# Gated linear attention with a cosine-gated MLP on one core: another order of the written-out steps behind the first 150

## The chip, the core and the metric

The kernel runs on one core of a Trainium2 chip. The metric is the device time of one execution in microseconds (us). A core has five queues that matter here: PE (matmuls), DVE, ACT and POOL (elementwise work; ACT also holds the tables for exp, ln and sine, POOL cannot read PSUM here) and SP, which only issues transfers. Each queue takes its instructions strictly in the order in which the program wrote them; between queues, semaphores make an instruction wait for its operands and for a free buffer. Matmul results go to PSUM, which the kernel divides into eight banks of 128 x 512 float32.

## The reference

For 4 batches, 8 heads, 768 steps and head width 48, with `state` of 48 x 48 per batch and head:

```python
for t in range(S):
    state = alpha[:, :, t, :, None] * state + np.einsum('bhd,bhe->bhde', k[:, :, t], v[:, :, t])
    y[:, :, t] = np.einsum('bhd,bhde->bhe', q[:, :, t], state)
...
h = x @ w_in            # x: y as 3072 tokens x 384;  w_in: 384 x 2048
g = h * np.cos(h)
return g @ w_out        # w_out: 2048 x 384
```

Inputs and output are float32; the kernel multiplies in bfloat16 and accumulates in float32.

## The kernel before, in words

The 3072 tokens are cut into 12 blocks of 256, J = 0 to 11; three blocks in a row belong to one batch. Inside a block there are two chunks of 128 tokens, and two tokens that follow each other lie on one partition (the index e = 0, 1). The recurrence is done chunk by chunk: with cumulative sums of ln(alpha), keys are scaled by exp(-sum) and queries by exp(sum); inside a chunk the masked products of queries and keys are applied to v, and a state handed from chunk to chunk adds the rest. The result is the MLP's input.

All work is cut into named steps, each for one J (and for one half, chunk or part). The prediction uses these names, "outer 2" being step outer of block 2, "evy 3 1" evy of block 3 with chunk 1, "m2 5 0 3" the second matrix of block 5, chunk 0, part 3:

- SP: `load a/k/q/v` (one input of a block, 384 KB; line 102), `vst` (four small transfers that stack v; 64 KB each), `out` (one output tile of 128 x 384).
- POOL: `mula` (product of neighbouring alphas), `castv` (v to bfloat16; line 219), `decay`, `state` (the decayed new state), and those of `sk` and `sq` (scaled keys and queries, half e) that have no `:D`.
- ACT: `sin` (cosine of a part of h), `eb` (a session: exp(-sum) and exp(sum) of both halves, then ln of the next block; line 203), and evictions marked as ACT's. Going from exp/ln to sine or back loads a table.
- DVE: `gate` (h times cosine), `mask` (scores times the mask), `add` (new state sum), `sub`, and the evictions and scalings marked `:D`.
- Evictions, on ACT or DVE: `evT` (transposed q and k of a chunk), `evy` (y), `evo` (output tile), `vev`.
- PE: `cums` (the sums), `trans` (32 transposes: keys, then queries), `scores` (chunk c), `outer` (state products; two chunks, one in a batch's last block), `yT`, `m1` (first matrix, part u of 4), `m2` (second matrix, chunk c, part p of 4), `vpe` (v restacked, blocks 0 to 2).

The data flow of a block is: loads, mula, ln, cums, sub and eb, sk and sq, trans, evT, scores, mask, yT, evy, then four times m1, sin, gate, then eight m2, two evo, two out. `outer` needs sk and castv; add and state follow it, and yT needs the state.

The order is written out by hand, not found by a scheduler at build time. `PLAN` (line 432) holds for each step and J a number, with a letter for the engine of an eviction or scaling; the steps are sorted by this number alone (line 513) and written in that order, each into its engine's queue. The numbers are not times that anything waits for. A step that stands early in a queue and has to wait holds up all that stands behind it in that queue.

Buffers set the other waits. Six PSUM banks form a ring "h" of three two-bank tiles (line 172), taken in turn by trans, scores, outer, yT and m1: the fourth of them waits until the first is evicted. Two more banks stand alone: "x" for cums and vpe, "o" for the output tiles of m2. Of input tiles there are three per tensor (four of alpha; `BUF`, line 45), of output tiles in SBUF four, so the fifth evo waits until the first tile is stored. All loads behind the first nine wait for the yT of block 1 (line 99), so that the weights come first.

Of the kernel before, what the change touches and what calls it, by code (L numbers as in the profile page):

```python
# [16 lines left out]
def kernel(  # L17
# [10 lines left out]
    nc = tc.nc  # L28
# [130 lines left out]
    def cums(J):  # L159
        if (J, 1) not in cums_ps:  # L160
            cums_ps[J, 1] = ps.tile([C, 512], FP, tag="x", name="cums", bufs=1)
# [10 lines left out]
    def two_banks(name):  # L172
        return ps.tile([C, 2, 512], FP, tag="h", name=name, bufs=3)

# [56 lines left out]
    def stack_v_pe(J, c):  # L231
        vs_ps[J, c] = ps.tile([C, 512], FP, tag="x", name="vs_ps", bufs=1)
        for e in range(2):
            r, o = slice(HC * c, HC * c + HC), slice(HC * e, HC * e + HC)
            nc.tensor.matmul(vs_ps[J, c][o, 0:HD].rearrange("s (h d) -> s h d", h=H), ident_bf[r, r],
                             vp_t[J % NV][r, e, :, 0:D], start=True, stop=True)
# [45 lines left out]
    def outer(J):  # L282
        n = 2 if J % NJB < NJB - 1 else 1
        kh, vp = kh_t[J % NQ], vp_t[J % NV]
        U_ps[J] = two_banks("U_ps")
        for p in range(NP):
            for e in range(2):
                for c in range(n):
                    r = slice(HC * c, HC * c + HC)
                    nc.tensor.matmul(  # L290
                        U_ps[J][:, c, 2 * p * D : 2 * (p + 1) * D].rearrange("r (a d) -> r a d", a=2),
# [7 lines left out]
    def add_state(J, c):  # L299
        n = 2 * J + c  # L300
        us = sb.tile([C, NP, 2, D], FP, tag="us", name="us", bufs=BUF["us"])
        s = U_ps[J][:, c, 0:HD].rearrange("r (p a d) -> r p a d", p=NP, a=2)
# [13 lines left out]
    def yT(J):  # L316
        y_ps[J] = two_banks("y_ps")
# [20 lines left out]
        for z, (c, g, i, l, r) in enumerate(todo):  # L338
            last = nc.tensor.matmul(y_ps[J][32 * g : 32 * g + 32, c, i * C : (i + 1) * C], l, r,  # L339
# [6 lines left out]
    def evict_y(J, c, copy):  # L346
        if J not in xT:
# [3 lines left out]
             in_=y_ps[J][:, c, 0 : KT * C].rearrange("r (i e t) -> r i e t", i=KT, e=2))  # L351
# [24 lines left out]
    def mlp2(J, c, part):  # L376
        if (J, c) == (NJ - 1, 1):
            if part == 0:

                o_ps[J, c] = [ps.tile([C, 512], FP, tag="x", name="o_last", bufs=1), two_banks("o_last")[:, 0]]  # L380
# [5 lines left out]
        if part == 0:  # L386
            o_ps[J, c] = ps.tile([C, 512], FP, tag="o", name="o_ps", bufs=1)
# [23 lines left out]
    def idle(n):  # L411
        if not idle_ps:
            idle_ps.append(ps.tile([C, 512], FP, tag="o", name="idle_ps", bufs=1))
# [7 lines left out]
        "mula": mul_a, "ln": ln, "cums0": cums0, "cums": cums, "sub": sub, "icp": icp, "exps": exps, "eb": session,  # L421
        "sk": lambda J, e, eng="POOL": scale_k(J, e, mults[eng]), "sq": lambda J, e, eng="POOL": scale_q(J, e, mults[eng]),
        "castv": cast_v, "vst": stack_v, "vpe": stack_v_pe,
# [3 lines left out]
        "m1": mlp1, "sin": cosine, "gate": gate, "m2": mlp2, "evo": lambda J, c, eng="ACT": evict_o(J, c, copies[eng]),  # L427
# [118 lines left out]
```

## Time and profile before

| what | us |
| --- | --- |
| median of 3 runs | 183.99 (183.46 to 184.06) |
| span of the profiled execution | 182.3 |
| PE busy | 175.4 |
| DVE busy | 134.8 |
| ACT busy, 18 table loads of 1.28 among it | 129.9 |
| POOL busy | 71.4 |
| bytes moved | 29.47 MB, mean 162 GB/s |

The profiled execution's own time is known as its span, from the first to the last instruction; it is 1.7 us less than the median of the runs. In the profile, a line such as `L389 PE MATMUL o_ps<-w,gsb` names the line of the kernel, the engine, the operation and the tiles (output, then inputs). The chain of waits lists, in order of time, start, length and what ran or was waited for. The timeline lists start, duration, engine, line, operation and tiles, and in brackets the idle time before it with what ended it. Matmuls overlap, so the durations of neighbours may not be added; the distance from start to start is what one takes from PE. In the trace PE names its tiles: `T_ps` is trans, `A_ps` scores, `U_ps` outer, `y_ps` yT, `h_ps` m1, `o_ps` m2; on the others `gsb` is gate, `c_sb` sin, `kh` and `qh` sk and sq, `xT` evy, `qkT` evT, `us` add, `un` state, `vp` castv.

### The profile page before, as it was taken

The page shows a single profiled execution, that of the slowest core. Times are in us where ns is not written, and L with a number is a line of the kernel's source. Part 1 is how long each engine was busy: PE and PEld are TensorE (multiplying, and loading weights), DVE is VectorE, ACT ScalarE, POOL GpSimd, SP SyncE. Part 2 cuts the span into 40 slices and gives each one's busy share as a digit, 9 for nine tenths or more (in the row PEclk, how much of TensorE's full clock was granted, in tenths as well). Part 3 has the DMA queues.
Part 4 walks back from the last instruction along what each step waited for, and adds up shares of the span by engine and source line. Part 5 has one row for each costly group of instructions (what it writes and reads, how often), then busy time and mean ns, then how long its engine had stood idle before and what let it go on. Part 6 is the DMA issues. An engine that isn't in the chain of part 4 may idle for free.

```text
span 182.3 us, 5756 instructions
## 1 busy us (share of the span) xinstructions
PE 175.4 (96%) x2467; PEld 132.6 (73%) x2470; DVE 134.8 (74%) x183; ACT 129.9 (71%) x169; POOL 71.4 (39%) x104
## 2 busy tenths in 40 slices
PE   7999899989999999998999999999999999999993
PEld 2455789746697877975799669686876796787872
DVE  7188878678879897599889886978688778363460
ACT  2837687998989999959578999838964174383331
POOL 5145830377777103734894298240720320100000
PEclk9999999999999999999999999999999999999999
DMA  5999999999989959996629905690052142010032
GB/s 148 261 261 220 199 215 221 273 260 265 248 184 283 249 132 295 289 277 202 147 63 229 273 18 166 155 233 0 4 110 83 45 109 81 4 43 4 0 129 86
DMA packets 57801, 29.47 MB, mean 162 GB/s; under 512 B 50992, under 2 KB 56496, under 8 KB 57776
## 3 DMA queue, kind: packets, MB, share of 16 engines
q1 hardware_dynamic: 56256, 25.86, 58.3%
q0 software_dynamic: 1376, 3.15, 9.3%
q8 instruction: 19, 0.31, 0.7%
q10 hardware_dynamic: 144, 0.10, 0.2%
q14 instruction: 6, 0.05, 0.1%
HBM read 25.17 MB, written 4.72 MB: 164 GB/s over the span
## 4 chain that ended last, share of the span: by engine, by line
PE 77%; ACT 11%; DVE 6%; DMA 2%; issue 2%; ACTq 0%
PE h_ps L360 29%; PE o_ps L389 28%; PE y_ps L339 5%; DVE gsb L371 5%; PE idle_ps L415 4%; ACT c_sb L366 3%; PE A_ps L273 3%; PE T_ps L259 3%; DMA a<-in_alpha_dram 2%; PE U_ps L290 2%; ACT L366 2%; PE o_last L383 1%; ACT L137 1%; ACT lna L142 1%; PE cums_h L156 1%
## 5 line engine op out<-in xcount | busy, mean ns | idle before, releaser
L371 DVE TENSOR_TENSOR gsb<-h_ps,c_sb 128x1024 bf16<-128x1024 f32 x48 | 58.2, 1222 | 20.8 <-ACT c_sb L366 19.4
L366 ACT ACTIVATE c_sb<-h_ps,halfpi 128x1024 bf16<-128x1024 f32 x48 | 53.3, 1115 | 26.7 <-PE h_ps L360 26.4
L389 PE MATMUL o_ps<-w,gsb 128*128 128x384 bf16 x368 | 67.1, 327 | 0.6 <-DVE o_sb L401 0.6
L360 PE MATMUL h_ps<-xT,w 128*128 128x256 bf16 x576 | 67.0, 273 | 0.3 <-issue 0.2
L360 PEld LDWEIGHTS <-w 128*128 128x128 bf16 x576 | 62.4, 114 | 2.5 <-DMA w<-in_moe_w_in_dram 0.3
L389 PEld LDWEIGHTS <-gsb 128*128 128x128 bf16 x368 | 33.9, 98 | 21.4 <-issue 1.1
L312 POOL TENSOR_TENSOR un<-us,c 128x384 bf16<-128x384 f32 x20 | 16.8, 838 | 46.2 <-DVE us L304 36.9
L278 DVE TENSOR_TENSOR A_sb<-A_ps,msk 128x1024 bf16<-128x1024 f32 x24 | 28.9, 1216 | 3.4 <-PE A_ps L273 3.4
L217 POOL TENSOR_TENSOR qh<-q,cp 128x384 bf16<-128x384 f32 x13 | 13.8, 1063 | 13.3 <-ACT cp L201 12.2
L213 POOL TENSOR_TENSOR kh<-k,icp 128x384 bf16<-128x384 f32 x15 | 14.9, 1007 | 2.4 <-ACT icp L193 1.0
L220 POOL CAST vp<-v 128x768 bf16<-128x768 f32 x12 | 9.9, 827 | 12.0 <-DMA v<-in_v_dram 12.0
L150 POOL TENSOR_TENSOR a<-a 128x384 f32<-128x384 f32 x9 | 9.0, 1003 | 10.1 <-DMA a<-in_alpha_dram 10.1
L142 ACT ACTIVATE lna<-a 128x768 bf16<-128x768 f32 x12 | 10.1, 844 | 3.5 <-DMA a<-in_alpha_dram 3.3
L415 PE MATMUL idle_ps<-zeros 128*128 128x512 bf16 x38 | 11.1, 439 | 1.4 <-DVE halfpi L77 1.2
L401 ACT COPY o_sb<-o_ps 128x384 f32<-128x384 f32 x13 | 6.2, 478 | 8.5 <-PE o_ps L389 8.5
L137 ACT ACT_TABLE_LOAD x9 | 11.5, 1283 | 0.9 <-PEq L530 0.7
L366 ACT ACT_TABLE_LOAD x9 | 11.5, 1283 | 0.2
L304 DVE TENSOR_TENSOR us<-U_ps,un 128x384 f32<-128x384 f32 x16 | 8.8, 551 | 3.8 <-POOL un L312 2.1
L265 ACT COPY qkT<-T_ps 128x1024 bf16<-128x1024 bf16 x10 | 9.8, 1016 | 1.9 <-PE T_ps L259 1.8
L217 DVE TENSOR_TENSOR qh<-q,cp 128x384 bf16<-128x384 f32 x11 | 6.8, 629 | 5.4 <-DMA q<-in_q_dram 5.3
L265 DVE COPY qkT<-T_ps 128x1024 bf16<-128x1024 bf16 x14 | 9.4, 680 | 1.2 <-PE T_ps L259 1.2
L273 PE MATMUL A_ps<-qkT 48*128 48x128 bf16 x192 | 9.0, 217 | 0.7 <-DVE gsb L371 0.5
(70 smaller groups left out, 156.6 us busy)
## 6 DMA issues: line engine op xcount, KB each, us to landing
a<-in_alpha_dram SPq DMA_DIRECT2D x12, 384.0 KB, 5.9
q<-in_q_dram SPq DMA_DIRECT2D x12, 384.0 KB, 6.1
k<-in_k_dram SPq DMA_DIRECT2D x12, 384.0 KB, 6.0
v<-in_v_dram SPq DMA_DIRECT2D x12, 384.0 KB, 6.3
out_dram<-o_sb SPq DMA_DIRECT2D x23, 192.0 KB, 3.5
vs<-vp SPq DMA_DIRECT2D x36, 64.0 KB, 2.8
w<-in_moe_w_in_dram POOLq DMA_DIRECT2D x2, 768.0 KB, 9.6
w<-in_moe_w_out_dram POOLq DMA_DIRECT2D x4, 384.0 KB, 8.7
```

The source lines that it names most:

```text
L137: nc.scalar.preload_act_table_set("natural_log_exp_and_others")
L213: eng.tensor_tensor(out=kh_t[J % NQ][:, e, :, 0:D], in0=kqv["k", J][:, :, e], in1=icp_, op=ALU.mult)
L217: eng.tensor_tensor(out=qh_t[J % NQ][:, e, :, 0:D], in0=kqv["q", J][:, :, e], in1=cp, op=ALU.mult)
L265: copy(out=qkT_sb[J][:, c], in_=T_ps[J][:, c].rearrange("r n e s -> r n (e s)"))
L273: nc.tensor.matmul(A_ps[J, c][:, a, p, :], qkT[r, c, NP + p, :], qkT[r, c, p, :], start=True, stop=True)
L278: nc.vector.tensor_tensor(out=A_sb[J][:, c].rearrange("s a p t -> s (a p) t"), in0=A_ps.pop((J, c)).rearrange("s a p t -> s (a p) t"), in1 ...
L312: nc.gpsimd.tensor_tensor(out=u, in0=U_sum.pop(n), in1=c2_sb[J][:, :, c].unsqueeze(3).to_broadcast([C, NP, 2, D]), op=ALU.mult)
L360: nc.tensor.matmul(h_ps[J, u][:, f, :], cols, xT[J][:, kk, :], start=(kk == 0), stop=(kk == KT - 1))
L366: nc.scalar.activation(out=c_sb[J, u], in_=h_ps[J, u], func=AF.Sin, bias=halfpi, scale=1.0)
L371: nc.vector.tensor_tensor(out=gsb[J][:, u * FW : (u + 1) * FW], in0=h_ps.pop((J, u)), in1=c_sb.pop((J, u)), op=ALU.mult)
L389: nc.tensor.matmul(o_ps[J, c][:, 0:DM], gsb[J][:, ft, c * C : (c + 1) * C], w2[:, ft], start=(ft == 0), stop=(ft == NF - 1))
L415: nc.tensor.matmul(idle_ps[0], zeros[:, 0:C], zeros, start=True, stop=True)
```

## The change

The order of the first 150 steps stays: up to about 40 us of the profile. Their numbers are new, ranks in place of the old ones. Behind them all steps are put in another order, on every queue, the loads and stores included. Three things go with it:

- Nine steps carry the mark `X` and use the other one of the two single banks: vpe 2 0 in "o"; m2 5 1, m2 7 1, m2 8 1, m2 9 0 and m2 10 1 in "x"; the state products outer 3, 10 and 11 leave the ring "h" and take "x" and "o" (block 11 only "x").
- 26 evictions change engine: twelve go from ACT to DVE (evT 3 1, 9 1, 10 0, 11 1; evy 2 1, 4 1, 8 1, 11 0; evo 1 1, 3 1, 6 0, 8 0) and fourteen from DVE to ACT (evT 6 1, 8 0, 10 1, 11 0; evy 5 1, 7 0, 7 1, 8 0, 9 0, 9 1; evo 4 1, 7 0, 8 1, 10 0).
- Two entries of w1 that did nothing are dropped.

No step is added or removed, and none changes its size. The start of the new part, on PE (old, then new):

```
old: m2 1 0 1, trans 2, outer 2, vpe 2 1, m2 1 0 2, vpe 2 0, scores 2 1, m2 1 0 3, cums 4, trans 3, scores 2 0,
     m2 1 1 0, m2 1 1 1, scores 3 0, m2 1 1 2, yT 2, scores 3 1, outer 3, m2 1 1 3, cums 5, m1 2 1 ...
new: trans 2, m2 1 0 1, m2 1 0 2, m2 1 0 3, outer 2, scores 2 1, vpe 2 0, vpe 2 1, scores 2 0, trans 3, cums 4,
     m2 1 1 0, m2 1 1 1, m2 1 1 2, m2 1 1 3, yT 2, scores 3 1, scores 3 0, outer 3, m1 2 0 ...
```

On POOL:

```
old: sk 2 1, castv 2, sk 3 1, sq 3 0, state 2 0, mula 5, castv 3, decay 3, sk 4 1, sk 4 0, ...
new: sk 2 1, sk 3 1, castv 2, decay 3, sq 3 0, mula 5, castv 3, state 2 0, sk 4 1, sq 4 0, ...
```

On SP, behind load v 3:

```
old: k4 q4 a6 a7 v4 vst3 k5 q5 out(0,1) out(0,0) q6 a8 a9 vst4 a10 out(1,1) q7 k6 v5 ...
new: k4 a6 q4 v4 vst3 k6 q5 k5 a9 v5 q6 out(0,0) a7 a8 out(0,1) vst4 v7 v6 out(1,0) k7 ...
```

The diff, with the reading sides of the changed tiles (`[:, c, ...]` becomes `[c][:, ...]`) and some rows of the plan left out:

```diff
--- before.py
+++ after.py
@@ -156,9 +156,12 @@
             nc.tensor.matmul(o, m.rearrange("p c i -> p (c i)"), lna_t[J % NL][:, i, :, 0:D], start=(i == 0),
                              stop=(i == len(mats) - 1))
 
-    def cums(J):
+    def one_bank(name, tag):
+        return ps.tile([C, 512], FP, tag=tag, name=name, bufs=1)
+
+    def cums(J, tag="x"):
         if (J, 1) not in cums_ps:
-            cums_ps[J, 1] = ps.tile([C, 512], FP, tag="x", name="cums", bufs=1)
+            cums_ps[J, 1] = one_bank("cums", tag)
         t = cums_ps[J, 1]
         lna = lna_t[J % NL]
         ne = 1 if J in both else 2
@@ -172,6 +175,12 @@
     def two_banks(name):
         return ps.tile([C, 2, 512], FP, tag="h", name=name, bufs=3)
 
+    def two(name, apart, n=2):
+        if apart:
+            return [one_bank(name, tag) for tag in ("x", "o")[:n]]
+        t = two_banks(name)
+        return [t[:, c] for c in range(2)]
+
     def cums0(J):
         t = two_banks("cums_h")
         for e in range(2):
@@ -228,8 +237,8 @@
 
     vs_ps = {}
 
-    def stack_v_pe(J, c):
-        vs_ps[J, c] = ps.tile([C, 512], FP, tag="x", name="vs_ps", bufs=1)
+    def stack_v_pe(J, c, tag="x"):
+        vs_ps[J, c] = one_bank("vs_ps", tag)
         for e in range(2):
             r, o = slice(HC * c, HC * c + HC), slice(HC * e, HC * e + HC)
             nc.tensor.matmul(vs_ps[J, c][o, 0:HD].rearrange("s (h d) -> s h d", h=H), ident_bf[r, r],
@@ -279,16 +288,16 @@
             out=A_sb[J][:, c].rearrange("s a p t -> s (a p) t"), in0=A_ps.pop((J, c)).rearrange("s a p t -> s (a p) t"),
             in1=msk.rearrange("s e2 t -> s (e2 t)").unsqueeze(1).to_broadcast([C, H, C]), op=ALU.mult)
 
-    def outer(J):
+    def outer(J, other=""):
         n = 2 if J % NJB < NJB - 1 else 1
         kh, vp = kh_t[J % NQ], vp_t[J % NV]
-        U_ps[J] = two_banks("U_ps")
+        U_ps[J] = two("U_ps", other, n)
         for p in range(NP):
             for e in range(2):
                 for c in range(n):
                     r = slice(HC * c, HC * c + HC)
                     nc.tensor.matmul(
-                        U_ps[J][:, c, 2 * p * D : 2 * (p + 1) * D].rearrange("r (a d) -> r a d", a=2),
+                        U_ps[J][c][:, 2 * p * D : 2 * (p + 1) * D].rearrange("r (a d) -> r a d", a=2),
                         kh[r, e, 2 * p : 2 * p + 2, :].rearrange("s h d -> s (h d)"),
                         vp[r, e, 2 * p : 2 * p + 2, 0:D], start=(e == 0), stop=(e == 1))
 
...
@@ -313,8 +322,8 @@
                                 in1=c2_sb[J][:, :, c].unsqueeze(3).to_broadcast([C, NP, 2, D]), op=ALU.mult)
         U_new[n] = u
 
-    def yT(J):
-        y_ps[J] = two_banks("y_ps")
+    def yT(J, other=""):
+        y_ps[J] = two("y_ps", other)
         qkT, A, vs = qkT_sb.pop(J), A_sb.pop(J), vs_t[J % NS]
         todo = []
         for i in range(KT):
...
@@ -373,18 +382,18 @@
 
     HALVES = [slice(0, DM // 2), slice(DM // 2, DM)]
 
-    def mlp2(J, c, part):
+    def mlp2(J, c, part, tag="o"):
         if (J, c) == (NJ - 1, 1):
             if part == 0:
 
-                o_ps[J, c] = [ps.tile([C, 512], FP, tag="x", name="o_last", bufs=1), two_banks("o_last")[:, 0]]
+                o_ps[J, c] = [one_bank("o_last", "x"), two_banks("o_last")[:, 0]]
             for z, cols in enumerate(HALVES):
                 for ft in range(part * NF // MP, (part + 1) * NF // MP):
                     nc.tensor.matmul(o_ps[J, c][z][:, 0 : DM // 2], gsb[J][:, ft, c * C : (c + 1) * C], w2[:, ft, cols],
                                      start=(ft == 0), stop=(ft == NF - 1))
             return
         if part == 0:
-            o_ps[J, c] = ps.tile([C, 512], FP, tag="o", name="o_ps", bufs=1)
+            o_ps[J, c] = one_bank("o_ps", tag)
         for ft in range(part * NF // MP, (part + 1) * NF // MP):
             nc.tensor.matmul(o_ps[J, c][:, 0:DM], gsb[J][:, ft, c * C : (c + 1) * C], w2[:, ft],
                              start=(ft == 0), stop=(ft == NF - 1))
...
@@ -418,86 +427,86 @@
     mults = {"DVE": nc.vector, "POOL": nc.gpsimd}
     steps = {
         "load": lambda J, nm: load(nm, J), "w1": load_w1, "w2": load_w2,
-        "mula": mul_a, "ln": ln, "cums0": cums0, "cums": cums, "sub": sub, "icp": icp, "exps": exps, "eb": session,
+        "mula": mul_a, "ln": ln, "cums0": cums0, "cums": lambda J, other="": cums(J, "o" if other else "x"), "sub": sub, "icp": icp, "exps": exps, "eb": session,
         "sk": lambda J, e, eng="POOL": scale_k(J, e, mults[eng]), "sq": lambda J, e, eng="POOL": scale_q(J, e, mults[eng]),
-        "castv": cast_v, "vst": stack_v, "vpe": stack_v_pe,
+        "castv": cast_v, "vst": stack_v, "vpe": lambda J, c, other="": stack_v_pe(J, c, "o" if other else "x"),
         "vev": lambda J, c, eng="DVE": evict_vs(J, c, copies[eng]), "decay": decay, "trans": trans,
         "evT": lambda J, c, eng="DVE": evict_T(J, c, copies[eng]), "scores": scores, "mask": mask, "outer": outer,
         "add": add_state, "state": decay_state, "yT": yT, "evy": lambda J, c, eng="ACT": evict_y(J, c, copies[eng]),
-        "m1": mlp1, "sin": cosine, "gate": gate, "m2": mlp2, "evo": lambda J, c, eng="ACT": evict_o(J, c, copies[eng]),
+        "m1": mlp1, "sin": cosine, "gate": gate, "m2": lambda J, c, part, other="": mlp2(J, c, part, "x" if other else "o"), "evo": lambda J, c, eng="ACT": evict_o(J, c, copies[eng]),
         "out": store, "idle": idle,
     }
 
 
     PLAN = {
-        "load a": "750 2205 4425 24496 25066 37693 43693 45193 55293 56793 62293 70470",
-        "load k": "3345 7425 31693 34693 40693 52193 64033 73545 85258 93648 94218 114101",
-        "load q": "2775 8925 25636 36193 42193 52763 54533 63463 72180 78488 96723 113531",
-        "load v": "5925 10425 33193 39193 46693 64693 71040 71610 94788 95358 117164 132675",
...
-        "eb": "- - - 39444 47093 58049 68038 83323 88148 102153 108001 126061",
-        "sk 0": "9160:D 14846:D 39112:D 41953:D 48949 58577 77428:D 89268 92888 110613 111733 130015",
-        "sk 1": "9909:D 13739:D 38528 41528 47999 59591:D 73470 88318 91938 107448 124627:D 130965",
...
-        "castv": "12160 17628 40028 46545 56778 71528 75880 90218 100558 104387 129245 144989",
...
-        "trans": "10624 16461 40648 44533 57020 68793 81884 90868 108663 115899 126133 137709",
-        "evT 0": "11929 17161:A 42626:A 45233:A 60041 70290:A 83189 93123 109551 117529:A 130540:A 139589",
-        "evT 1": "11324 18286 41348 46163:A 58511 71220:A 82584 91568 110631 116599:A 131821 138409:A",
...
-        "scores 1": "12159 19026 43154 48677 59649 82364 85716 101272 118725 125913 134675 140410",
...
-        "outer": "14769 19786 41128 48897 68243 85386 81554 104346 116599 118945 140630 151540",
...
-        "yT": "18046 23626 47792 56295 71422 88605 89395 107778 123407 138284 149254 161470",
...
-        "evy 1": "18876 25109 49345 58036:D 72782 89595:D 90795 110156:D 124397 139114:D 150367 162953",
...
-        "m2 1 0": "35362 45328 65536 77529 86551 104771 117324 129332 141275 154809 166285 173504",
...
-        "evo 0": "34574:D 44322 62603 73475 85575 103280:D 116004 128413:D 140515 153925:D 165167:D 176969",
-        "evo 1": "38637:D 54119 68348:D 81659 92173:D 108601:D 123512 133462 144087:D 157621 171423 178295:D",
-        "out 0": "53933 66193 79058 75045 109831 110431 116564 149019 141075 173183 172583 177529",
...
+        "load a": "10 30 60 980 1020 1410 1750 2500 2520 2230 3070 3970",
+        "load k": "50 170 1170 1280 1540 2210 1970 3040 3440 3490 4690 5040",
+        "load q": "40 240 1040 1330 1840 2110 2370 3090 3750 4170 5220 4610",
+        "load v": "100 270 1220 1460 1950 2340 2940 2830 3940 3150 4250 4660",
...
+        "eb": "- - - 1480 1910 2300 2710 3280 3720 4290 4760 4990",
+        "sk 0": "250:D 510:D 1450:D 1500:D 2060 2320 2790:D 3630 4230 4320 4840 5510",
+        "sk 1": "260:D 440:D 1430 1510 1920 2460:D 3190 3670 4050 4640 4910:D 5340",
...
+        "castv": "350 660 1560 1740 2530 3010 3370 3420 4700 4110 4600 5030",
...
+        "trans": "280 610 1520 1730 2250 2770 3320 3800 4750 4770 5570 5560",
+        "evT 0": "330 650:A 1580:A 1870:A 2400 2850:A 3400 3890 4820:A 4860:A 5630 5700:A",
+        "evT 1": "300 690 1530 1800 2310 2900:A 3340:A 3900 4870 4780 5690:A 5650",
...
+        "scores 1": "340 730 1660 1900 2390 3360 3580 4330 4980 5320 5720 5710",
...
+        "outer": "500 790 1610 2000:X 2750 3260 3610 4190 4710 4790 5530:X 5900:X",
...
+        "yT": "680 950 1890 2240 2890 3700 3770 4390 5110 5500 5960 6110",
...
+        "evy 1": "720 1030 1930:D 2350:D 2950:D 3740 3790 4480 5130:D 5600 6060 6170",
...
+        "m2 1 0": "1300 1780 2640 3170 3620 4340:X 4850 5100:X 5610:X 6150 6490:X 6650",
...
+        "evo 0": "1270:D 1630 2590 3120 3540 4470:D 4740:D 5470 6120:D 6400:D 6560 6670",
+        "evo 1": "1440:D 1880:D 2760:D 3350:D 3850 4520:D 5090 5520 5840 6360 6630 6720:D",
+        "out 0": "2490 3030 3220 4150 4620 4800 5590 5850 6200 6420 6600 6700",
...
     }
-    IDLE = [(1201, 9), (6413, 2), (7383, 14), (11727, 1), (12377, 4), (15372, 5), (16939, 5), (20459, 1)]
+    IDLE = [(20, 9), (120, 2), (160, 14), (310, 1), (370, 4), (550, 5), (640, 5), (840, 1)]
 
     order = []
     for key, line in PLAN.items():
@@ -505,7 +514,7 @@
         for J, word in enumerate(line.split()):
             if word != "-":
                 t, _, eng = word.partition(":")
-                args = [J] + [int(x) if x.isdigit() else x for x in rest] + [{"A": "ACT", "D": "DVE", "P": "POOL"}[x] for x in eng]
+                args = [J] + [int(x) if x.isdigit() else x for x in rest] + [{"A": "ACT", "D": "DVE", "P": "POOL", "X": "other bank"}[x] for x in eng]
                 order.append((int(t), len(order), kind, args))
     for t, n in IDLE:
         order.append((t, len(order), "idle", [n]))
```

More of the change, by code (lines that the diff above doesn't have):

```diff
@@ L301, in add_state @@
         us = sb.tile([C, NP, 2, D], FP, tag="us", name="us", bufs=BUF["us"])
-        s = U_ps[J][:, c, 0:HD].rearrange("r (p a d) -> r p a d", p=NP, a=2)
+        s = U_ps[J][c][:, 0:HD].rearrange("r (p a d) -> r p a d", p=NP, a=2)
         if n % (2 * NJB) > 0:
@@ L338, in yT @@
         for z, (c, g, i, l, r) in enumerate(todo):
-            last = nc.tensor.matmul(y_ps[J][32 * g : 32 * g + 32, c, i * C : (i + 1) * C], l, r,
+            last = nc.tensor.matmul(y_ps[J][c][32 * g : 32 * g + 32, i * C : (i + 1) * C], l, r,
                              start=(c, g) not in begun, stop=(c, g, i) not in outs[z + 1 :], skip_group_check=True)
@@ L350, in evict_y @@
         copy(out=xT[J][:, :, c * C : (c + 1) * C].rearrange("r i (t e) -> r i e t", e=2),
-             in_=y_ps[J][:, c, 0 : KT * C].rearrange("r (i e t) -> r i e t", i=KT, e=2))
+             in_=y_ps[J][c][:, 0 : KT * C].rearrange("r (i e t) -> r i e t", i=KT, e=2))
     h_ps, c_sb, o_ps, o_sb = {}, {}, {}, {}
@@ L412, in idle @@
         if not idle_ps:
-            idle_ps.append(ps.tile([C, 512], FP, tag="o", name="idle_ps", bufs=1))
+            idle_ps.append(one_bank("idle_ps", "o"))
         for _ in range(n):
```

94 rows, old and new, of the table PLAN are left out of this document.

## The prediction

> **What bounds the kernel now.** I read the busy table and the slices first, then the chain of waits in order of time, then the timelines of PE, DVE, ACT and POOL around the places where that chain leaves PE.
>
> ```profile
> span 182.3 us, 5756 instructions
> PE 175.4 (96%) x2467; PEld 132.6 (73%) x2470; DVE 134.8 (74%) x183; ACT 129.9 (71%) x169; POOL 71.4 (39%) x104
> PE   7999899989999999998999999999999999999993
> PEclk9999999999999999999999999999999999999999
> ```
>
> PE is the bound, at full granted clock, in every slice behind the start. So a new order can win only two things on PE: waits, and what PE loses between unlike matmuls. The chain shows the second:
>
> ```profile
> 35.87 1.30 PE o_ps L389 x8
> 37.17 0.16 PE cums L156
> ...
> 45.20 1.41 PE o_ps L389 x8
> 46.60 0.33 PE A_ps L273 x8
> 46.93 0.76 PE o_ps L389 x4
> ...
> 68.82 0.23 PE A_ps L273 x8
> 69.04 0.47 PE T_ps L259 x32
> ```
>
> Eight `o_ps` matmuls take 1.30 us ahead of another full-array matmul, 1.41 ahead of scores; eight scores take 0.23 ahead of transposes, 0.33 ahead of `o_ps`. Going from full-array work (cums, m1, m2) to half-row work (trans, scores, outer) or to the column-split yT, or back, costs 0.10 us; among trans, scores and outer it costs nothing. The first is the wait:
>
> ```profile
> 81.83 1.22 DVE gsb L371
> 83.05 0.04 issue
> 83.09 0.40 PE A_ps L273 x8
> ```
>
> **Floor.** Behind step 149, PE runs from 40.03 to 179.27 us in the profile. I laid each PE step at its undisturbed length by the PE timeline (m1 1.31, m2 0.65, trans 0.48, scores 0.23, outer 0.35 or 0.15, yT 0.79 or 0.63, cums 0.26) plus 0.095 for each change of shape. What exceeds it in before by more than 0.05 is waiting: 0.65 between trans 6 and scores 5 1; 0.49 around scores 8 0, outer 8 and cums 11; 0.19 each around scores 6, scores 11 0 and outer 2; 0.15 behind cums 5; 0.11 at m1 3 1. Together 2.0 us.
>
> **The change, part by part.**
>
> Changes of shape: counted along both plans behind step 149, 59 become 50. Nine fewer at 0.10: **-0.9 us**, directly on PE, and nothing hides it.
>
> The waits. I follow each engine's queue in the new order with the durations of the trace (DVE from start to start: gate and mask 1.17, evT 0.60, sk and sq 0.50, other 0.47; ACT: sin 1.11, table load 1.28, a session of icp, exps and ln 2.45).
>
> First new wait, at the seam. POOL's sk 3 1 now stands ahead of castv 2. It needs load k 3:
>
> ```profile
> 40.04 0.82 POOL L220 CAST vp<-v 128x768 bf16<-128x768 f32 x1 [0.37 <-DMA v<-in_v_dram]
> 41.56 1.00 POOL L213 TENSOR_TENSOR kh<-k,icp 128x384 bf16<-128x384 f32 x1 [0.70 <-ACT cp L201]
> ```
>
> (ACT had long written icp; it was the load.) The front, and with it this landing, stays. So sk 3 1 ends at 42.56 and castv 2 at 43.4; outer 2 wants PE at 42.74: **+0.65**. Behind it on POOL come decay 3 (0.21) and sq 3 0 (1.06 to 1.35), until 44.7 to 44.9; the query half of trans 3 is due at 44.7: **+0.15** (0 to 0.3). On DVE, sk 3 0 too waits for k 3 and holds up evT 2 1 until 43.0, ahead of the delayed scores 2 1: no cost. At yT 2 the new order is then 0.1 us behind the old; m1 2 starts at 50.1 in place of 50.26, with cums 5 (0.26) still to come.
>
> From 49 to 72 us DVE runs almost without a gap: it takes evT 3 1, evo 1 1, evy 2 1 and later evy 4 1 and evo 3 1 over from ACT. Margins of PE's needs here: mask 3 0 before m1 2 2 0.1; evy 3 1 before m1 3 2 0.1 to 0.2; gate 3 2 before m1 3 3 0.1; gate 3 3 before trans 5 0.1; mask 4 0 (behind evo 2 1, add 4 0 and sk 6 0) before yT 4 -0.2 to 0.1. I take **+0.2** for yT 4, between 0 and 0.5 for the row.
>
> The DMA queue: loads k 6, q 5, k 5, a 9, v 5, q 6 now go ahead of the first store, out 0 0, and output tiles have four buffers, so evo 2 0 (ACT, turn at 64.1) waits for it. In before, 4.2 MB landed from 47.8 (k 4) to 65.7 us (a 9), 0.234 MB/us. By that row the 4.0 MB up to out 0 0 have landed at 64.9; at the 0.25 of the page's better slices at 63.8. ACT then runs up to 0.8 us late; gate 3 3 is DVE's turn only at 67.7 and hides most of it, evT 5 and evy 4 0 pass on **+0.2** (0 to 0.4). The later loads have slack: k 5 by 59 for sk 5 0 at 58.5 (POOL alone), a 7 by 67 for ln 7 at 70, q 8 by 86 for 90. vst 5, 6, 8 and 9 land over 3 us ahead of their yT, vst 4 some 2 us.
>
> The old wait at 83: the two DVE multiplications of J=6 there (0.88 and 1.18) now stand earlier; gate 4 3 ends at 82.1, scores 5 1 wants it at 82.5: **-0.65**. At m2 4 0 0 the new order leads by 0.3, at m1 6 1 by 0.6.
>
> From 100 to 121: outer 7 finds gate 6 0 0 to 0.1 ahead, m1 7 3 finds evy 7 1 and gate 6 2 0.1 to 0.2 ahead. Sessions 10 and 11 follow each other without a sin, so ACT loads its table 16 times instead of 18: 2.57 us less on ACT, off the chain but just where its chain stood:
>
> ```profile
> 105.41 1.28 ACT L366 ACT_TABLE_LOAD   x1
> 106.71 1.11 ACT L366 ACTIVATE c_sb<-h_ps,halfpi 128x1024 bf16<-128x1024 f32 x1
> 107.84 1.28 ACT L137 ACT_TABLE_LOAD   x1
> ```
>
> With add 8 0 done at 116.0 for outer 9 at 116.4 and exps 10 done at 116.5 for cums 11 at 117.5, **-0.49** goes. Behind 121, m2 of J=5, 7, 8, 9 and 10 alternates between the two single banks, and outer 10 and 11 leave the h ring: all releases I followed come 0.1 to 2 us early (closest: evo 7 1 before outer 10). The small old waits go as well: **-0.8**. The last m2 and its split store keep their form; tail 3.1 us as now.
>
> For ten places with margins of 0.2 or less I add **+0.5** (0 to 1.0: each missed by 0.1 on the mean).
>
> Sum: -0.9 -0.65 -0.49 -0.8 +0.65 +0.15 +0.2 +0.2 +0.5 = **-1.1 us**: a span of 181.2. The profiled span is 1.7 us under the median of the runs; what lies around it is unchanged, so 183.99 - 1.1 = **182.9 us**.
>
> A place where a rule may speak against this: in before DVE's kh took 0.91 us beside POOL's kh, which had begun first and kept its 1.00; alone it takes 0.55 to 0.62. The new order releases sk 3 0 (DVE) and sk 3 1 (POOL) by the same landing. The Trainium skill, "SBUF — State Buffer", section "Who interferes with whom", says that a DVE instruction with two SBUF inputs and a GpSimd one that reads SBUF lock each other out, and whoever issues first holds the ports for its whole length. The row agrees (DVE blocked some 0.3 us). By the row POOL keeps its 1.00 us, by the rule, if DVE is first, it starts a multiplication later; that is the third rival.
>
> **Rivals.**
> 1. Slower: the first store. If out 0 0 lands at 67 or later, sin 3 1 and sin 3 3 fall 2 us behind, DVE has nothing to hide it with, and gate 3 3, trans 5 and all behind it move. Past 65 us each us costs about 0.9; at 66.9 it undoes the forecast's gain and 0.55 more, at 67.5 it gives 184.0 - 1.1 + 2.2 = 185.1. For it: six loads ahead of it in one queue. Against: 0.234 MB/us held through a stretch with the same kinds of transfer.
> 2. DVE becomes the bound from 49 to 72 us: with each of its 28 instructions at its full mean instead of the distance of starts, 0.08 more, 2.2 us; half of that gives 184.0, all of it 185.1. Against: consecutive starts on the timeline (57.99, 58.47, 59.06, 59.53).
> 3. sk 3 0 goes first and holds up sk 3 1 by 0.55: outer 2 waits 1.2; 183.5.
> 4. The orders are equal for PE: ten tight places each pass on 0.2, and what is saved between shapes is spent waiting; 184.0. That the shapes are regrouped at all is plain from the order.
> 5. Better: no margin fails and the landing is early, -0.9 -1.95 +0.65 +0.15 = -2.05: 181.9.
>
> **How the numbers follow.** Forecast 0.48 (182.3 to 183.4), rival 5 0.13, rivals 3 and 4 with the weak half of 2 0.19, rival 1 0.12, full rival 2 0.08. Faster by over 0.3% (0.55 us, about what can be told from no change here, with runs 183.46 to 184.06): 0.48 + 0.13 = 0.61, with a rest of 0.01 from rival 3; within: 0.18; slower: 0.20. Range: down to 181.8 (rival 5), up to 184.9, in rivals 1 and 2, which leaves about 0.15 out; the forecast alone spans 182.3 to 183.4.
>
> **What would show it.** PE: outer 2 with a wait of 0.6 behind POOL's castv near 43; no idle PE at the J=6 transposes; some nine fewer 0.1 us gaps; m1 7 2 some 1 us earlier than an equal amount of work in before. ACT: 16 table loads. Wrong if evo 2 0 starts after 66, or if DVE shows no idle time from 49 to 72 while PE waits for masks and gates by more than 0.5 in sum.

## The result and the profile after

The changed kernel takes 188.07 us (median of 4 runs, 187.82 to 188.69) against 183.76 (183.46 to 184.06) for the kernel before, run beside it. The ratio is 1.0236, with a 95% interval of 1.0211 to 1.0261: slower by 2.4 per cent, where 182.9 us and a gain were forecast. The profiled execution took 187.99 us with a span of 186.2, so what lies around the span is 1.8 us (1.7 before). Of the runs below, two were in a slower state (197.73 us in the first experiment, 185.95 in the eleventh) and are left out of the ratios.

The head of the page of the changed kernel, with the share of the chain of waits by engine:

```profile
span 186.2 us, 5765 instructions
PE 175.4 (94%) x2470; PEld 133.4 (72%) x2470; DVE 132.9 (71%) x181; ACT 128.4 (69%) x169; POOL 72.5 (39%) x104
PE   7899999987999997999899999989999999999993
PEclk9999999999999999999999999999999999999999
...
PE 66%; ACT 15%; DMA 8%; DVE 3%; issue 2%; POOL 2%; SPq 1%; DVEq 0%
```

PE is busy for the same 175.4 us at nearly the same granted clock (0.998, before 1.000); DVE and ACT have a little less to do than before (134.8 and 129.9). No engine became the bound. All that was added is idle time on PE: six of its slices behind the first show a 7 or an 8, where before shows three 8s and no 7.

The same ledger as in the prediction (each PE step at its undisturbed length, 0.095 for each change of shape) gives where it lies. Waiting is what the distance holds beyond that, gaps under 0.05 us included. Behind step 149 before has 59 changes of shape and 2.54 us of waiting (the prediction's 2.0 counted only gaps over 0.05), after has 49 and 7.28. That is -0.95 + 4.74 = +3.8; the distance from the first of these steps to the last grew from 138.38 to 142.17, by 3.79. The larger waits of after are:

| PE step, at us | wait | who was late |
| --- | --- | --- |
| outer 2, 43.6 | 0.92 | castv 2 on POOL |
| m1 2 0, 50.8 | 0.52 | evy 2 0 (ACT) behind evy 2 1 (DVE) |
| yT 4, 73.4 | 1.04 | the bank of trans 5, both halves on ACT |
| m1 4 1, 75.7 | 0.42 | evy 4 1 (DVE) behind evy 4 0 (ACT) |
| scores 6 1 and outer 6, 89.1 | 1.10 | evT 6 0 (DVE) behind evT 6 1 (ACT) |
| m1 6 1, 95.7 | 0.56 | evy 5 0 and 6 0 (DVE) behind evy 5 1 and 6 1 (ACT); 0.51 stays without the pairs (fourth run) |
| m1 7 2, 125.3 | 0.87 | add on DVE, late through evT 8 1 (DVE) behind evT 8 0 (ACT) |

Together 5.4; cums 4, m1 3 3, m1 8 3, scores 10 0 and yT 10 add 0.9. The two old waits that the forecast struck out, at scores 5 1 and at outer 8 with cums 11, are gone.

The list of waits of after shows a kind of line that the prediction's walk through the queues did not have: an eviction that waits for the eviction of the other half of the same tile. Columns: engine, line, what is waited for, us in total, times, the longest.

```profile
DVE qkT L274 <- ACT qkT L274: 3.4, 2, 2.6
DVE xT L359 <- ACT xT L359: 3.1, 2, 2.4
ACT qkT L274 <- DVE qkT L274: 2.5, 3, 1.0
ACT xT L359 <- DVE xT L359: 2.2, 3, 1.4
```

The list of waits of before has one such line:

```profile
ACT xT L350 <- DVE xT L350: 0.3, 1, 0.3
```

The two halves of `qkT` or `xT` have nothing to do with each other in the data. But they are read from one two-bank PSUM tile, and where ACT evicts one half and DVE the other, the program as built makes the eviction that stands second in the written order wait until the first has *ended*. What it hangs on was read from built programs alone, and no run here shows it: with `qkT` as two SBUF tiles the wait is still there, with the PSUM tile of evT 6, or of evy 2, as two one-bank tiles it is not. Before has six such split pairs, one of them in the front; the 26 changed engines make fourteen, thirteen of them behind the front. (The expectations of the first and fourth run count twelve behind the front and ten mended; by the plans it is thirteen and twelve.)

The timeline of after around one of them, evT 6:

```profile
82.52 1.28 ACT L137 ACT_TABLE_LOAD   x1
...
83.98 0.56 DVE L410 COPY o_sb<-o_ps 128x384 f32<-128x384 f32 x1
...
85.40 0.84 ACT L142 ACTIVATE lna<-a 128x768 bf16<-128x768 f32 x1
86.14 1.01 ACT L274 COPY qkT<-T_ps 128x1024 bf16<-128x1024 bf16 x1
87.18 0.69 DVE L274 COPY qkT<-T_ps 128x1024 bf16<-128x1024 bf16 x1 [2.64 <-ACT qkT L274]
...
87.79 1.22 DVE L287 TENSOR_TENSOR A_sb<-A_ps,msk 128x1024 bf16<-128x1024 f32 x1
...
89.06 0.40 PE L282 MATMUL A_ps<-qkT 48*128 48x128 bf16 x8 [0.70 <-DVE A_sb L287]
```

DVE is free at 84.54 and stands still for 2.64 us; all but the first 0.3 of it lies behind the end of the transposes, at 84.86. ACT, which has the half that is written first, is in the middle of a session (table load, exps, ln) and comes to it only at 86.14. So one engine's session becomes the other engine's idle time, the mask behind it is late, and PE waits at scores 6 1.

### The profile page after: what moved, and what is told of

It reads as the page before. It is cut to its first block, busy times and chain, and to the rows that moved or that the text cites. A ratio compares the mean times of both kernels' runs of the same rounds, so it can differ in the third digit from the quotient of the medians.

```text
span 186.2 us, 5765 instructions
## 1 busy us (share of the span) xinstructions
PE 175.4 (94%) x2470; PEld 133.4 (72%) x2470; DVE 132.9 (71%) x181; ACT 128.4 (69%) x169; POOL 72.5 (39%) x104
## 4 chain that ended last, share of the span: by engine, by line
PE 66%; ACT 15%; DMA 8%; DVE 3%; issue 2%; POOL 2%; SPq 1%; DVEq 0%
PE h_ps L369 30%; PE o_ps L398 19%; DMA a<-in_alpha_dram 7%; PE y_ps L348 6%; PE idle_ps L424 4%; ACT L137 3%; ACT qkT L274 3%; ACT c_sb L375 2%; ACT cp L210 2%; PE A_ps L282 2%; ACT lna L142 2%; ACT xT L359 2%; PE o_last L392 1%; ACT icp L202 1%; PE U_ps L299 1%
## 5 line engine op out<-in xcount | busy, mean ns | idle before, releaser
L398 PE MATMUL o_ps<-w,gsb 128*128 128x384 bf16 x368 | 66.2, 326 | 0.6 <-DVE o_sb L410 0.6
L398 PEld LDWEIGHTS <-gsb 128*128 128x128 bf16 x368 | 34.5, 98 | 21.3 <-issue 0.9
L226 POOL TENSOR_TENSOR qh<-q,cp 128x384 bf16<-128x384 f32 x13 | 13.3, 1028 | 15.2 <-ACT cp L210 13.8
L222 POOL TENSOR_TENSOR kh<-k,icp 128x384 bf16<-128x384 f32 x15 | 15.4, 1026 | 6.5 <-ACT icp L202 4.5
L424 PE MATMUL idle_ps<-zeros 128*128 128x512 bf16 x41 | 11.8, 428 | 1.2 <-DVE halfpi L77 1.2
L359 ACT CAST xT<-y_ps 128x384 bf16<-128x384 f32 x16 | 8.8, 598 | 5.8 <-PE y_ps L348 3.5
L229 POOL CAST vp<-v 128x768 bf16<-128x768 f32 x12 | 10.8, 906 | 3.0 <-DMA v<-in_v_dram 3.0
```

Of the source, the lines that this page charges most:

```text
L222: eng.tensor_tensor(out=kh_t[J % NQ][:, e, :, 0:D], in0=kqv["k", J][:, :, e], in1=icp_, op=ALU.mult)
L226: eng.tensor_tensor(out=qh_t[J % NQ][:, e, :, 0:D], in0=kqv["q", J][:, :, e], in1=cp, op=ALU.mult)
L398: nc.tensor.matmul(o_ps[J, c][:, 0:DM], gsb[J][:, ft, c * C : (c + 1) * C], w2[:, ft], start=(ft == 0), stop=(ft == NF - 1))
L424: nc.tensor.matmul(idle_ps[0], zeros[:, 0:C], zeros, start=True, stop=True)
```

## The experiments

All kernels ran at least four times beside the kernel before, whose medians in the five groups of runs were 183.67 to 184.16; ratios are to the kernel before of the same group, so medians of different groups can differ by some tenths for that reason alone. The expectations name three theories. P: the split pairs. O: the new order itself loads DVE and ACT badly, whatever engine evicts. B: the bank given to each tile is at fault. A fourth suspect is the seam at 43 us.

**1. The engines of the old kernel in the new order (first run).** Each eviction gets the engine that it had before; twenty-six entries of this kind:

```diff
-        "evo 1": "1440:D 1880:D 2760:D 3350:D 3850 4520:D 5090 ...
+        "evo 1": "1440:D 1880 2760:D 3350 3850:D 4520:D 5090 ...
```

> The new order with its bank marks, but every eviction on the engine that it had before. Theory P (pairs): when ACT and DVE each empty one half of the same two-bank PSUM tile, the program makes the second wait for the first, and the new order has 12 such pairs behind step 149 where the old has 5; PE waits next to them in the trace of the new kernel add up to 3.9 us (0.52 at m1 2 0, 0.42 at m1 4 1, 1.1 at scores 6, 0.56 at m1 6 1, 0.87 at m1 7 2, 0.19 at m1 8 3, 0.29 at scores 10 0). By P some 2.5 to 3.5 us go: 184.6 to 185.6. Theory O (the order itself overloads DVE and ACT): no gain, since five evictions return to ACT early and DVE gets others late: 187.5 to 188.5. Theory B (banks): nothing, 188.

Measured 194.72 us (192.52 to 197.73), ratio 1.053 (1.0447 to 1.0612). By the ledger PE waits 13.7 us: 2.0 at cums 11, 1.7 at m2 4 0 0, 1.5 at m1 7 3, 1.2 at m1 2 0. A miss for every theory: six split pairs in place of fourteen, and far slower. At m2 4 0 0 the trace shows why: evo 3 1, on ACT again, stands behind the session for block 7 and starts only at 87.77, with bank "o" occupied until then. That evictions on an engine that is elsewhere at that point make the other waits too is likely and not shown.

**2. The new engines in the old order (second run).** The reverse.

> The old order and banks with the engines of the new kernel's evictions, the other part alone. P: slower than before by 1 to 3 us (8 more split pairs, each up to 0.6 to 1 us where PE waits for the second half): 185 to 187. O and B: as before within 0.5 us, 183.3 to 184.3, since the load of each engine hardly changes.

Measured 189.14 us (188.81 to 189.27), ratio 1.0278 (1.0254 to 1.0302), 7.4 us of waiting: 1.6 at m1 7 3, 1.1 at cums 8, 0.95 at m1 2 1, others at outer 8 and scores 8 1. The direction was as P has it, the size larger. The lines of split pairs are there in the old order too: 4.7, 3.4, 3.1 and 1.4 us in the list of waits. The two runs together say only that order and engines belong together: neither half of the change can be priced by itself.

**3. One split pair (third run): evT 6 1 goes to DVE, behind evT 6 0.**

```diff
-        "evT 1": "300 690 1530 1800 2310 2900:A 3340:A 3900 ...
+        "evT 1": "300 690 1530 1800 2310 2900:A 3405 3900 ...
```

> The new kernel with only evT 6 1 moved from ACT to DVE, behind evT 6 0: one split pair less. P: the waits at scores 6 1 and outer 6 (0.86 and 0.24) go, up to 0.5 us comes back at trans 7 or m1 6 1: 187.0 to 187.5. O: no change (188.0), DVE having 0.6 us more to do.

Measured 186.85 us (186.70 to 186.96), ratio 1.0157 (1.0140 to 1.0174). The timeline of this kernel at the same place:

```profile
84.76 1.29 DVE L274 COPY qkT<-T_ps 128x1024 bf16<-128x1024 bf16 x2 [0.36 <-PE T_ps L268]
...
85.97 1.22 DVE L287 TENSOR_TENSOR A_sb<-A_ps,msk 128x1024 bf16<-128x1024 f32 x1
...
87.82 0.62 PE L282 MATMUL A_ps<-qkT 48*128 48x128 bf16 x16
88.28 0.51 PE L299 MATMUL U_ps<-vp,kh 64*128 64x96 bf16 x16
```

DVE evicts both halves in 1.29 us at once, in place of standing still for 2.64; the mask starts at 85.97 in place of 87.79, and PE runs the sixteen scores and outer 6 without a break. The 1.10 us of waiting went, and the median fell by 1.2 (by 1.4 against the kernel before of each group): this pair was worth its wait in full.

**4. Twelve split pairs on one engine (fourth run).** evT 2, 6, 9, 10 and evy 2, 4, 6, 8 wholly on DVE, evT 3, 8, 11 and evy 5 on ACT, four of these evictions moved by a few places. Of the edit, two rows:

```diff
-        "evT 0": "330 650:A 1580:A 1870:A 2400 2850:A 3400 3890 4820:A 4860:A 5630 5700:A",
+        "evT 0": "330 650:A 1535 1870:A 2400 2850:A 3400 3890 4820:A 4785 5630 5700:A",
...
-        "evy 1": "720 1030 1930:D 2350:D 2950:D 3740 3790 4480 5130:D 5600 6060 6170",
+        "evy 1": "720 1030 1930:D 2350:D 2950:D 3740 3790:D 4480 5130:D 5600 6060 6170",
```

> The new kernel with both halves of a block on one engine in ten of its split pairs (evT 2, 6, 9, 10 and evy 2, 4, 6, 8 on DVE, evT 3, 8, 11 and evy 5 on ACT; four steps move beside their partner; 2 split pairs are left, one of them in the front). Unlike giving back all old engines, the evo stay where the new order has them. P (the second engine waits for the first): the waits at m1 2 0 (0.3 of 0.52), m1 4 1 (0.2 of 0.42), scores 6 and outer 6 (1.1), m1 6 1 (0.2 of 0.56), m1 7 2 (0.87) and scores 10 (0.3) shrink: -2 to -3 us, 185.0 to 186.0 beside 188.0. O (the load of DVE and ACT in this order): DVE takes 3 us more work between 41 and 95 us, so no gain or a loss, 188 to 189.

Measured 185.51 us (185.19 to 185.65), ratio 1.008 (1.0065 to 1.0095): 2.5 us less than the changed kernel, as P has it and O does not. PE's waiting fell from 7.28 to 4.34, and of the lines of split pairs, 11.2 us in after, two of 0.4 are left in the list. This is the largest cause. What is left sits at outer 2 (0.76), yT 4 (1.04), m1 6 1 (0.51), m1 2 0 (0.35) and m1 4 1 (0.26). The last three follow an eviction so closely in the new order that they wait for it on one engine too: 1.1 us together, in place of 1.5.

**5. The seam (fifth run): castv 2 ahead of sk 3 1.**

```diff
-        "castv": "350 660 1560 1740 2530 ...
+        "castv": "350 660 1505 1740 2530 ...
```

> The new kernel with POOL's castv 2 ahead of sk 3 1 again. The wait at outer 2 (0.92 us in the trace of the new kernel) goes; if it is on the path as the forecast said, 187.0 to 187.4; if the waits behind it take it up, 187.8 to 188.2. trans 3 may wait longer for sq 3 0 (0.1 to 0.3).

Measured 187.64 us (187.57 to 187.68), ratio 1.0199 (1.0177 to 1.0221), 0.4 less than the changed kernel. Outer 2's wait of 0.92 went; 1.3 us further on another took the place of a part of it:

```profile
42.70 0.42 PE L299 MATMUL U_ps<-vp,kh 64*128 64x96 bf16 x6
...
44.04 0.36 PE L244 MATMUL vs_ps<-vp,ident_bf 64*64 64x384 bf16 x4 [0.61 <-ACT o_sb L410]
```

vpe 2 0 waits for bank "o", which evo 1 0 on ACT empties late: it stands behind evT 2 0, and that behind DVE's evT 2 1, a split pair again. With the twelve pairs mended and castv 2 moved (sixth run):

> The pairs and castv 2, with the ring as the build gives it out: 0.3 to 1.0 us above the run with fixed turns if the wait at yT 4 stays; equal to it if the ring is given out otherwise once the evictions have moved.

Measured 185.09 us (184.55 to 185.26), ratio 1.0054 (1.0035 to 1.0074). Against the fourth run the gain of the move is 0.4 again by the medians, though the single runs overlap; the ledger has the same, 3.92 us of waiting against 4.34, with 0.76 gone at outer 2 and 0.37 new at trans 3.

**6. The ring of banks.** In the timeline of after, yT 4 starts late although another tile of the ring is free:

```profile
70.93 1.22 DVE L287 TENSOR_TENSOR A_sb<-A_ps,msk 128x1024 bf16<-128x1024 f32 x1
71.40 1.93 ACT L274 COPY qkT<-T_ps 128x1024 bf16<-128x1024 bf16 x2
...
73.37 0.52 PE L348 MATMUL y_ps<-qkT,un 128*32 128x128 bf16 x24 [0.97 <-ACT qkT L274]
```

The oldest tile in the ring is that of scores 4 0, which mask 4 0 had emptied at 72.15. But the banks are chosen when the program is built, and yT 4 was given those of trans 5, which ACT evicted until 73.33. The seventh run gives the three banks strictly in turn behind the front, the eighth does so on top of the sixth:

```diff
-        return ps.tile([C, 2, 512], FP, tag="h", name=name, bufs=3)
+        return ps.tile([C, 2, 512], FP, tag=slot(), name=name, bufs=1)
```

> The new kernel with the two-bank ring taken strictly in turn behind the front; as built, yT 4 got the buffer of trans 5, which ACT empties until 73.3, instead of that of scores 4 0, which DVE had emptied at 72.15. P: only the wait at yT 4 (1.04 us) goes, a part of it comes back at m1 4 1: 187.0 to 187.6. B (buffers given out in another turn than the plan's are the main cost): 185 to 186.

Measured 187.74 us (187.60 to 190.0), ratio 1.0234 (1.0172 to 1.0295): 0.3 less than the changed kernel by the medians, no gain that can be told from these runs. The 1.04 at yT 4 went, and scores 6 0, at the split pair of evT 6, then waited 1.54 in place of the 1.10 there; the sum of waiting is 7.00 us against 7.28.

> The same, with castv 2 ahead of sk 3 1 and the ring of two-bank tiles taken strictly in turn. P with the two other causes (seam 0.9, ring 1.0 at yT 4): all of the new waits but 0.5 to 1 us are gone: 182.5 to 184.0, that is as before or up to 0.8% faster. O: 186.5 or more.

Measured 184.29 us (184.14 to 184.84, 10 runs), ratio 1.0009 (0.9983 to 1.0035). Against the sixth run this is 0.8 us by the medians. How much of it is the banks is not settled: the two profiled executions took 184.51 and 184.55, and the sums of waiting are 3.67 and 3.92, since 0.92 went at yT 4 and 0.54 came at trans 3. By the ledger the banks are worth 0.25 here and 0.28 with the pairs in place. All three causes mended, the new order is equal to the old one.

**7. Three more moves for the waits that were left (ninth run).**

```diff
-        "sk 0": "250:D 510:D 1450:D 1500:D 2060 2320 2790:D ...
+        "sk 0": "250:D 510:D 1450:D 1500:D 2060 2320 2815:D ...
-        "m2 0 2": "1210 1590 2380 2880 ...
+        "m2 0 2": "1210 1590 2380 2951 ...
-        "m2 1 3": "1400 1830 2720 3210 3680 ...
+        "m2 1 3": "1400 1830 2720 3210 3805 ...
-        "decay": "480 800 1340 1620 ...
+        "decay": "480 800 1340 1635 ...
```

> The order of after with pairs mended, castv 2 ahead of sk 3 1 and the ring taken in turn, plus three moves of steps: the last part of m2 4 1 behind cums 9 and ahead of m1 6 1 (cover for evy 5 and evy 6, about 0.4 us of wait at m1 6 1); mask 4 0 ahead of sk 6 0 on DVE and the third part of m2 3 0 behind evy 4 1 (about 0.45 at m1 4 1 and yT 4); decay 3 behind sq 3 0 on POOL (about 0.15 at trans 3). If what is left of waiting in this order is the lack of PE work between an eviction and its reader, the three give 0.7 to 1.0 us: 183.3 to 183.6, 0.3 to 0.5 per cent under before. If a wait that is covered only comes back at the next step, as with the ring in turn alone, it stays at 184.0 to 184.5.

Measured 184.57 us (184.05 to 185.24, 11 runs), ratio 1.005 (1.0035 to 1.0065). A miss: no faster than the eighth run. The waits at m1 4 1 (0.36) and m1 6 1 (0.50) did go, but scores 5 0, which m2 3 0 2 had covered, now waits:

```profile
73.12 0.40 PE L287 MATMUL A_ps<-qkT 48*128 48x128 bf16 x8 [0.73 <-DVE us L318]
73.45 1.47 PE L403 MATMUL o_ps<-w,gsb 128*128 128x384 bf16 x8
```

The sum of waiting is 3.69 us against 3.67.

**8. Are the old kernel's waits worth their size? (tenth to thirteenth run.)** The forecast had counted 1.14 us for the two large old waits. These runs take them away in the old order: sk 6 0 into an idle gap of DVE; then outer 8 (with add 8 0 and state 8 0) behind the two parts of m2 6 1 as well.

```diff
-        "sk 0": "9160:D 14846:D 39112:D 41953:D 48949 58577 77428:D ...
+        "sk 0": "9160:D 14846:D 39112:D 41953:D 48949 58577 76280:D ...
...
-        "outer": "14769 19786 41128 48897 68243 85386 81554 104346 116599 ...
+        "outer": "14769 19786 41128 48897 68243 85386 81554 104346 118700 ...
```

> The order of before with one DVE step moved: sk 6 0 from behind gate 4 1 (77.67 in the profile of before) to ahead of it, into DVE's idle 0.94 us at 75.6. If the prediction's term of 0.65 for the wait between trans 6 and scores 5 1 was right as a price on PE, the last gate of block 4 no longer waits for DVE's two multiplications, the wait goes and nothing takes its place: 183.1 to 183.4 against 183.8, 0.2 to 0.4 per cent faster. If a wait taken away there only comes back at a later step, as it did in the new order, the time stays within 0.2 of before.

Measured 183.70 us (183.17 to 184.30, 12 runs), ratio 0.9982 (0.9968 to 0.9996).

> The same, and outer 8 behind the two parts of m2 6 1 in place of ahead of cums 11 (add 8 0 and state 8 0 behind it), so that matmuls cover the 0.3 us that outer 8 waits for a bank. If both old waits are worth their size: another 0.3 to 0.45, 182.7 to 183.1, 0.5 per cent under before. If the shift of add 8 0 on DVE and of state 8 0 on POOL makes yT 8 late: no gain over the first kernel, or a loss.

Measured 183.42 us (183.05 to 185.95, 12 runs), ratio 0.9972 (0.9957 to 0.9987): the lowest ratio of the study, a little faster than both kernels, but 0.5 us where the two waits measure 1.14. In the tenth run PE has no gap at scores 5 1, and the profile shows 0.5 of the 0.65 again further on:

```profile
82.57 0.39 PE L273 MATMUL A_ps<-qkT 48*128 48x128 bf16 x8
82.89 2.77 PE L389 MATMUL o_ps<-w,gsb 128*128 128x384 bf16 x16
...
89.15 0.28 PE L339 MATMUL y_ps<-A_sb,vs 128*32 128x128 bf16 x5
89.75 0.55 PE L339 MATMUL y_ps<-A_sb,vs 128*32 128x128 bf16 x25 [0.32 <-DMA vs<-vp]
```

The step that waits is yT 5, not yT 6 as the expectation of the twelfth run calls it: the plan has yT 5 first, and vst 6 ahead of vst 5. The last part of the stacked v of block 5, the last of eight transfers in a row on SP, landed at 89.61; PE stood ready for it at 89.2, in the middle of yT 5. In before it landed at 89.29 and PE came to it at 89.75. So PE was 0.5 us earlier and the transfer 0.3 later: the old wait had hidden a limit that lay less than 0.5 us behind it. Then vst 5 was put ahead of vst 6, and both ahead of out 2 1 and load q 9:

```diff
-        "vst": "- - - 48193 58293 82758 80258 ...
+        "vst": "- - - 48193 58293 79200 80258 ...
```

> Before with sk 6 0 early, and on SP vst 5 ahead of vst 6 and both ahead of out 2 1 and load q 9. In the run with sk 6 0 alone the 0.65 at scores 5 1 went, and 0.5 of it came back at yT 6, whose stacked v (vst 6, then vst 5, eight transfers issued one behind the other) landed at 89.6. If that transfer was a second limit that the old wait had hidden, landing it 1.5 us or more earlier gives yT 6 without a wait and the rest of the 0.65: 183.1 to 183.4. If something else holds block 6 there (mask 5 0, the state), yT 6 or its neighbours wait on: 183.6 to 183.8.

Measured 183.51 us (183.19 to 183.96, 12 runs), ratio 0.9989 (0.9974 to 1.0004). In the profile the wait in yT 5 is gone and the sum of waiting falls to 1.81 us (2.39 in the tenth run, 2.54 in before); the times do not show it.

> The same with outer 8 behind the two parts of m2 6 1 as well. There the waits at outer 8 and cums 11 (0.48) went and 0.33 of it came back at m1 7 2, which waits for the bank of outer 8. If waits add up once the hidden limits are gone: 182.8 to 183.2, the lowest of all; if not, no better than the kernel with sk 6 0 and the stacked v alone.

Measured 183.42 us (183.33 to 184.09, 12 runs), ratio 0.9983 (0.9970 to 0.9995): no better than the eleventh run. In these profiles small waits change place from run to run (this one shows 0.63 at m1 5 0, which the others do not), and the spans of 23 runs of the kernel before beside it go from 181.6 to 182.7 with a median near 181.9; the profiled 182.3 is one draw. So 0.65 us seen in one profile need not be 0.65 in a median. How much of the difference is this and how much are hidden limits stays open.

A kernel with the new order and without the marks `X` was not tried, so the marks have no price of their own here.

## Why the prediction was wrong

The measured time is 5.2 us above the forecast. By the medians the runs account for 3.7 of it: split pairs 2.5 (fourth run), castv 2 behind sk 3 1 another 0.4 (sixth against fourth), the bank order 0.8 (eighth against sixth). The ledger divides nearly the same sum otherwise, 2.9, 0.4 and 0.25; the pairs are the largest part in both. The rest, 1.4, is the distance of the eighth run from 182.9. It is waiting too: the forecast's terms leave 2.54 - 1.94 + 1.7 = 2.3 us of it, the eighth run has 3.67, with 0.91 at trans 3 and 0.36, 0.36 and 0.50 at m1 2 0, m1 4 1 and m1 6 1.

**The step that failed** is the walk "I follow each engine's queue in the new order with the durations of the trace", with the margins read from it. It lets an instruction start when its engine is free and its operands are there. The waits between the two evictions of one PSUM tile were not in it, though twelve evictions were written down as going to DVE and fourteen to ACT. "Scores 5 1", "m1 6 1" (forecast to lead by 0.6; waited 0.56), "m2 4 0 0" and the ten thin margins were all computed without them. At m1 6 1 that is not the whole of it, since 0.51 stayed in the fourth run; what the walk missed there beside the pairs is open. The term "+0.5 for ten places" should have been about 4: the waits of the table without outer 2 and yT 4 make 3.5, and 0.6 of the smaller ones belong to it. The pairs are the larger part of that, not all: 1.1 us stayed at m1 2 0, m1 4 1 and m1 6 1 with both halves on one engine, where the step follows its eviction too closely.

Point by point:

- **Changes of shape, -0.9.** Right in number (59 to 49, one more than counted) and, by the ledger that closes to within 0.1 us, in price.
- **Outer 2, +0.65.** It waited 0.92. The timeline of after at the seam:

```profile
41.37 0.56 DVE L222 TENSOR_TENSOR kh<-k,icp 128x384 bf16<-128x384 f32 x1 [0.27 <-ACT cp L210]
41.41 1.38 POOL L222 TENSOR_TENSOR kh<-k,icp 128x384 bf16<-128x384 f32 x1 [1.86 <-ACT cp L210]
...
42.73 0.82 POOL L229 CAST vp<-v 128x768 bf16<-128x768 f32 x1
...
43.61 0.41 PE L299 MATMUL U_ps<-vp,kh 64*128 64x96 bf16 x6 [0.85 <-POOL vp L229]
```

  The place and the cause (castv 2 behind sk 3 1 behind load k 3) were right. The size was that of rival 3: DVE's sk 3 0 began 0.04 us ahead of POOL's sk 3 1, kept its 0.56, and POOL's took 1.38 where it takes 1.00 alone. The rival's price of 1.2 was a little high, since POOL lost 0.38 and not 0.55. The rule of the Trainium skill, "SBUF — State Buffer", section "Who interferes with whom", agrees with this row: the order of issue decides which of the two blocks.
- **Trans 3, +0.15.** No wait there; cums 4 behind it waited 0.17.
- **yT 4, +0.2.** It waited 1.04, and not for mask 4 0, as was forecast: that ended at 72.15, and the wait was for trans 5's banks until 73.33. The statement that the ring is taken "in turn" was wrong, and with it "all releases I followed" wherever it was used.
- **The first store, +0.2, and rival 1.** The term was right: out 0 0 landed at 64.69 (forecast 64.9), evo 2 0 started at 64.72, and m1 3 3 waited 0.16. So rival 1 did not come.
- **Rival 2, DVE as the bound.** It did not come. From 49 to 72 us DVE was busier than before, 21.25 of 23 us against 20.61, but it still had idle time, and the waits of PE there come to 0.7, 0.52 of it at m1 2 0 behind a split pair. Over the whole span DVE had less to do than before.
- **Old waits, -0.65, -0.49, -0.8.** The two large ones are gone in the trace. The tenth to thirteenth runs suggest, for the old order, that such a wait is worth less than its size; for the new order no run prices them. Table loads: 16, as forecast.
- **Tail and clock.** Unchanged, as forecast.
- **Rival 4** (what is saved between shapes is spent waiting) was the nearest in kind, but with 0.2 for each of ten places, where single ones cost 0.5 to 1.1. No rival had the split pairs, so no case reached 188.

## What to carry to other kernels

Before an eviction or any other reader of a shared tile is moved to another engine, look for the tile's other readers: if a second engine reads the same PSUM tile, the program may tie the two together, and a session on one engine becomes idle time on the other. The list of waits shows it as a line with the same tile on both sides and two engines (`DVE qkT <- ACT qkT`), and one such line, of 0.3 us, was there in the profile before. A wait that is struck out of a forecast should be followed to the next limit behind it (a transfer, another bank). And a small gain should be read twice, from repeated times and from the sum of waiting: for the banks the medians gave 0.3 alone and 0.8 behind the other two changes, the ledger 0.28 and 0.25.

## What the runs showed beside that

- Which of two engines issues first by 0.04 us decides a lasting cost: DVE's 0.56 and POOL's 1.38 in one order. In the eighth run, some microseconds on, POOL's sq 3 0 went first and kept its 1.00, and DVE's sq 3 1 beside it took 1.29 in place of 0.56; DVE's add behind it was late, and trans 3, which needs the bank that this add empties, waited 0.91:

```profile
43.00 1.00 POOL L231 TENSOR_TENSOR qh<-q,cp 128x384 bf16<-128x384 f32 x1
43.12 1.29 DVE L231 TENSOR_TENSOR qh<-q,cp 128x384 bf16<-128x384 f32 x1
```

- A tile that takes its buffer from a pool of three got one that was emptied 1.2 us later (73.33) than another of the same pool (72.15).
